# Strassen's block products for the FFN up product of the last eight token tiles, with the converted weights kept in DRAM

## The chip, the core and the metric

The kernel runs on one core of a Trainium2 chip. The metric is the device time of one execution in microseconds (us). Four engines compute: TensorE (PE in the profile: matrix products, 128 x 128 weights against up to 512 columns, results in eight PSUM banks), VectorE (DVE), ScalarE (ACT) and GpSimd (POOL). All DMAs are issued from SyncE's queue (SP). Each engine works through its own instructions in the order in which they stand and waits at semaphores for the others.

## The reference

Attention with capped scores for 48 heads, then one FFN over 1792 tokens (14 tiles of 128), with a residual:

```python
scores = cap * np.tanh(scale * np.matmul(q, k.transpose(0, 1, 3, 2)) / cap)
attn = np.exp(scores - np.max(scores, axis=-1, keepdims=True))
attn = attn / (np.sum(attn, axis=-1, keepdims=True) + 1e-09)
x = np.matmul(attn, v)                     # (4, 12, 448, 64), all fp32
x = x.transpose(0, 2, 1, 3).reshape(4, 448, 768)
xn = (x - mean) / np.sqrt(var + 1e-06) * g_ln
out = x + np.maximum(xn @ w_ch1, 0.0) @ w_ch2   # 768 -> 3072 -> 768
```

q, k and v are fp32; the two weights are float64 and come as pairs of 32-bit words.

## The kernel before

**Products in two halves.** The FFN products need fp32 accuracy from a faster fp32r product, so each operand is split into a high part h and a rest l, and each product is three matmuls: h with h, l with h, h with l (L818 to L820 for the up product, L843 to L845 for the down product).

**Tiles and groups.** The hidden layer is worked through in 24 chunks of 128 (`fc`), the 768 input columns in 6 chunks (`CC`). The 14 token tiles are in four groups: A0 and A1 (3 tiles, 384 columns each), C0 and C1 (4 tiles, 512 columns each). `up` makes one chunk of the hidden layer for one group (18 matmuls), takes it out of PSUM with a ReLU on ACT (L823) and makes its rest on DVE (L825). `down` multiplies 2 or 4 such chunks with the second weight into a bank of 128 x 384, and DVE adds the bank to the tokens (L847).

**Weights.** Every chunk of either weight is one DMA of 768 KB (L764); ACT or POOL scale it (L769, L770), POOL and DVE put the words together (L773, L776, L778), ACT and DVE make h and l (L372, L379). This is done twice for each of the 48 chunks: `ffn(0, ...)` runs over the 24 chunks for A0 and, from chunk 8 on, also A1, while the attention of the later heads is still going on; `ffn(1, ...)` runs over them again for C0 and C1, and for A1 in the first 8.

**Norm.** `norm` makes, for one group, the statistics (L705, L707), the inverse root (L717 to L719), the normed tokens xn (L726), their transposes on PE (L734), and the h and l parts (L739, L743).

**What sets the order.** Every operation is recorded with an engine, a cost, a due time and the buffers that it needs. `Order.emit` goes through time with the given costs and lets each engine take the earliest due operation that is ready and whose buffers are free. So each engine's order is fixed when the kernel is built. Buffers of a kind are slots: a PSUM `bank` has 8, and a tag limits how many of them one use may hold.

## Time and profile before

| | |
|---|---|
| runs shown | 923.58 us median of 3: 920.82, 923.58, 1266.4 |
| profiled execution, first to last instruction | 920.0 us; its own device time is not listed, the shortest run is 0.8 us above this span, the median 3.6 us |
| busy | PE 902.9 us (98%), DVE 608.0 (66%), ACT 388.5 (42%), POOL 131.3 (14%) |
| DMA | 109.59 MB, mean 119 GB/s, 37.9% of 16 engines |
| granted TensorE clock | 0.999 |

A share of busy time is an average. The rows by stretch show which engine has no time left in which part, and the waits which engine another one stands still for. Busy PE time is a union of overlapping matmuls, so what one matmul costs in a row of them is read from the count in a stretch, not from its own duration.

### The profile page before, as it was taken

What the parts mean: (1) busy time and instruction counts of PE and PEld (TensorE: products, weight loads), DVE (VectorE), ACT (ScalarE), POOL (GpSimd) and SP (SyncE); (2) the same over time, 40 slices, a digit from 0 to 9 for tenths busy, and PEclk for the clock granted to TensorE, in tenths of its full rate; (3) what the DMA queues carried; (4) which work ended last, traced back from release to release, by engine and by line L of the source; (5) the groups of instructions that cost most, each with busy time, mean ns of one, the idle gap of its engine ahead of it and who ended that gap; (6) DMA issues with size and microseconds to landing.
All of it is one profiled execution on the core that took longest, in us unless ns stands there. A gap on an engine that the chain in (4) does not pass through costs nothing.

```text
span 920.0 us, 12465 instructions
## 1 busy us (share of the span) xinstructions
PE 902.9 (98%) x4886; PEld 746.8 (81%) x4886; DVE 608.0 (66%) x926; ACT 388.5 (42%) x553; POOL 131.3 (14%) x162
## 2 busy tenths in 40 slices
PE   8899999999999999999999999999999999999997
PEld 5337674877787777879989898989889899899896
DVE  2998788987775848569989373736473573663622
ACT  7865777765555574732442212111330430330400
POOL 2434111211110101011211010100020110110100
PEclk9999999999999999999999999999999999999999
DMA  9781655475434343236333130302241241240212
GB/s 230 217 238 50 188 166 153 122 229 137 151 116 158 107 130 117 92 104 260 117 107 110 54 112 28 110 30 82 78 144 63 71 170 35 97 144 35 70 61 80
DMA packets 34260, 109.59 MB, mean 119 GB/s; under 512 B 5008, under 2 KB 17808, under 8 KB 34192
## 3 DMA queue, kind: packets, MB, share of 16 engines
q1 hardware_dynamic: 34192, 108.71, 37.9%
q8 instruction: 40, 0.66, 0.3%
q14 instruction: 28, 0.23, 0.1%
HBM read 100.04 MB, written 8.65 MB: 118 GB/s over the span
## 4 chain that ended last, share of the span: by engine, by line
PE 90%; DVE 5%; ACT 2%; DMA 1%; issue 1%; POOL 1%; DVEq 0%; ACTq 0%
PE bank L818 13%; PE bank L843 13%; PE bank L845 12%; PE bank L819 12%; PE bank L844 12%; PE bank L820 12%; PE bank L575 5%; PE bank L424 5%; DMA raw<-in_w_dram 1%; PE bank L734 1%; PE bank L591 1%; ACT e L609 1%; DVE l L379 1%; PE bank L546 1%; PE bank L506 1%
## 5 line engine op out<-in xcount | busy, mean ns | idle before, releaser
L843 PE MATMUL bank<-h,hh 128*128 128x384 f32 x672 | 225.7, 336 | 0.2 <-DVE r L535 0.2
L845 PE MATMUL bank<-h,hl 128*128 128x384 f32 x672 | 224.6, 334 | 0.0
L844 PE MATMUL bank<-l,hh 128*128 128x384 f32 x672 | 224.5, 334 | 0.0
L847 DVE TENSOR_TENSOR x<-bank,x 128x384 f32<-128x384 f32 x272 | 146.5, 551 | 100.2 <-PE bank L845 99.5
L773 POOL TENSOR_SCALAR raw<-raw 128x768 f32<-128x768 f32 x96 | 104.3, 1087 | 622.3 <-ACT c L769 621.9
L372 ACT ACTIVATE h<-c 128x768 fp32r<-128x768 f32 x88 | 73.8, 843 | 186.6 <-PE bank L845 99.6
L843 PEld LDWEIGHTS bank<-h,hh 128*128 128x128 f32 x672 | 126.1, 188 | 6.8 <-issue 2.7
L844 PEld LDWEIGHTS bank<-l,hh 128*128 128x128 f32 x672 | 126.1, 188 | 0.2
L845 PEld LDWEIGHTS bank<-h,hl 128*128 128x128 f32 x672 | 126.1, 188 | 0.0
L823 ACT ACTIVATE hh<-bank 128x384 fp32r<-128x384 f32 (+1 forms) x96 | 52.2, 543 | 174.8 <-PE bank L820 174.7
L776 DVE SCALAR_TENSOR_TENSOR raw<-raw 128x768 int32<-128x768 int32 x96 | 92.6, 965 | 38.2 <-POOL raw L773 37.9
L769 ACT ACTIVATE c<-raw 128x768 f32<-128x768 f32 x88 | 79.8, 908 | 87.5 <-DMA raw<-in_w_dram 44.6
L818 PE MATMUL bank<-hC,h 128*128 128x512 f32 x288 | 113.9, 396 | 0.0
L825 DVE SCALAR_TENSOR_TENSOR hl<-bank,hh 128x384 fp32r<-128x384 f32 (+1 forms) x96 | 59.4, 619 | 82.3 <-ACT hh L823 82.1
L820 PE MATMUL bank<-hC,l 128*128 128x512 f32 x288 | 113.8, 395 | 0.0
L819 PE MATMUL bank<-lC,h 128*128 128x512 f32 x288 | 113.7, 395 | 0.0
L379 DVE TENSOR_TENSOR l<-c,h 128x768 fp32r<-128x768 f32 x96 | 94.0, 981 | 28.6 <-ACT h L372 26.9
L778 DVE SCALAR_TENSOR_TENSOR c<-c,raw 128x768 int32<-128x768 int32 x96 | 102.2, 1064 | 2.3
L818 PE MATMUL bank<-hA,h 128*128 128x384 f32 x288 | 100.6, 349 | 0.2 <-ACT e L609 0.2
L819 PE MATMUL bank<-lA,h 128*128 128x384 f32 x288 | 97.5, 339 | 0.0
L820 PE MATMUL bank<-hA,l 128*128 128x384 f32 x288 | 97.4, 338 | 0.0
L609 ACT ACTIVATE e<-bank,sc 128x448 f32<-128x448 f32 x144 | 81.1, 647 | 25.9 <-PE bank L575 25.9
(76 smaller groups left out, 914.0 us busy)
## 6 DMA issues: line engine op xcount, KB each, us to landing
raw<-in_w_dram SPq DMA_DIRECT2D x96, 768.0 KB, 4.5
d<-in_kq_dram SPq DMA_DIRECT2D x48, 224.0 KB, 6.2
v<-in_v_dram SPq DMA_DIRECT2D x24, 227.5 KB, 5.5
out_dram<-x SPq DMA_DIRECT2D x28, 192.0 KB, 1.9
v<-in_v_dram SPq DMA_DIRECT2D x24, 195.0 KB, 5.4
x<-xd SPq DMA_DIRECT2D x8, 384.0 KB, 7.8
xd<-a SPq DMA_DIRECT2D x21, 128.0 KB, 3.4
xd<-a SPq DMA_DIRECT2D x6, 64.0 KB, 2.0
```

What stands on the lines that cost most here:

```text
L379: self.eng(e).tensor_tensor(out=out, in0=in_, in1=high.bitcast(F32), op=ALU.subtract)
L609: add({"A": ACTP(S) + 93}, lambda e: nc.scalar.activation(tiles[p].ap[:, k, j] if p < 2 else er.ap[:, k], z.ap[:, :S], AF.Tanh, scale=self ...
L773: add(on("sg", G=POOL1(DM), V=VEC1(DM)), lambda e: nc.gpsimd.tensor_scalar(f(hi()), f(hi()), 0.0, 1.0, op0=ALU.mult, op1=ALU.mult) if e == ...
L776: add({"V": VEC2(DM)}, lambda e: nc.vector.scalar_tensor_tensor(hi(), lo(), 29, hi(), op0=ALU.logical_shift_right, op1=ALU.bitwise_or), wr ...
L778: add({"V": VEC2(DM)}, lambda e: nc.vector.scalar_tensor_tensor(c.ap, c.ap, 3, hi(), op0=ALU.logical_shift_left, op1=ALU.bitwise_or), read ...
L818: nc.tensor.matmul(ps.ap[:, :n], lhsT=w1h.ap[:, wc], rhs=xh.ap[:, c], start=(c == 0), stop=False)
L819: nc.tensor.matmul(ps.ap[:, :n], lhsT=w1h.ap[:, wc], rhs=xl.ap[:, c], start=False, stop=False)
L820: nc.tensor.matmul(ps.ap[:, :n], lhsT=w1l.ap[:, wc], rhs=xh.ap[:, c], start=False, stop=(c == CC - 1))
L843: nc.tensor.matmul(o, lhsT=h[0].ap[:, mc], rhs=w[0].ap[:, hc], start=(f == 0), stop=False)
L844: nc.tensor.matmul(o, lhsT=h[0].ap[:, mc], rhs=w[1].ap[:, hc], start=False, stop=False)
L845: nc.tensor.matmul(o, lhsT=h[1].ap[:, mc], rhs=w[0].ap[:, hc], start=False, stop=(f == last))
L847: add({"V": VEC2(HALF)}, lambda e, t=t, ps=ps, hc=hc: nc.vector.tensor_tensor(out=self.x(t)[:, hc], in0=ps.ap[:, :HALF], in1=self.x(t)[:, ...
```

## The change

The groups C0 and C1 get their up product as a 2 x 2 block product: two hidden chunks by two halves of the 768 inputs by two token groups. Strassen's form in Winograd's variant makes it from 7 block products of 9 matmuls (`stage`, 12 times) where the plain form has 8. The seven token operands (named 11, 21, 22, 1, 2, 3, 4, tiles `X1` to `X7` in that order) are made once in `blocks`; the seven weight operands are made in each stage from fp32 weights. Partial results are taken aside by ACT (`aside`, L1054) and added on DVE (`plus`, L1059). Each stage is followed by its own down product over 2 chunks instead of 4.

Each weight chunk is converted once. Its fp32 form is written to DRAM (`keep`, L839) and read back (`fetch`, L844) where it is needed again: for the first 8 chunks of A1, which get a phase of their own between the two others, and for the 12 stages. C's tokens are normed in place and read from DRAM a second time for the residual. The statistics of the tokens that go to DRAM are taken piece by piece in `finish` (L584) before they are stored. The pools are laid out anew, so the order comes out differently in the attention part too.

```diff
--- before.py
+++ after.py
 HALF = DM // 2
 NA = 6
 GROUPS = dict(A0=(0, 3), A1=(3, 3), C0=(6, 4), C1=(10, 4))
-FBS = [2, 4]
-HBS = [4, 8]
-W2S = [3, 4]
+FB = 2
+HB = 4
 WRAP = 8
+SLOTS = 8
+KH = CC // 2
+NE = KH * 128
+TOK = 512
 VEC1 = lambda n: 60 + 0.75 * n
...
-    w1=20000, w2=3000, evac=2000, cstep=15600, cnorm=10000, load=20000, zpad=3000, rush=30000, ahead=20000,
+    w1=20000, w2=3000, evac=2000, bstep=6300, cstep=31200, cnorm=10000, load=20000, zpad=3000, rush=30000, ahead=20000,
+    again=12000, down=16000, chunk=8000, blocks=4000,
...
+                add({"V": 330}, lambda e, dst=dst, tl=tl, p=p: nc.vector.bn_stats(
+                    self.stats.ap[p, tl % SLOTS, h0 // GROUP], dst()), reads=writes,
+                    writes=[(self.stats, tl % SLOTS, h0 // GROUP, p.start)], due=due)
...
+        self.keep((w, fc), lambda: f(c.ap), [c], due)
+        self.tail = op
         return h, l
-    def ffn(self, gi, hp, t0, step):
-
-        fc0 = 0
-        while fc0 < FC:
-            early = fc0 < WRAP
-            keys = (["A0"] if early else ["A0", "A1"]) if gi == 0 else (["C0", "C1", "A1"] if early else ["C0", "C1"])
-            n = FBS[0] if early else FBS[gi]
-            end = {"A0": FC, "A1": WRAP if gi else FC * (WRAP == 0), "C0": FC, "C1": FC}
-            due2 = t0 + (fc0 + 0.5 * n) * step
+    def again(self, w, fc, due, tag="cq"):
+
+        nc, add = self.nc, self.add
+        c = self.buf("wp", tag, [128, DM], F32)
+        op = self.fetch((w, fc), lambda: c.ap, [c], due, [self.gate, *self.rear])
+        self.fetched.append(op)
+        h, l = self.pair(w, fc)
+        self.split(h, l, c, due)
+        return h, l
+
+    def keep(self, key, ap, reads, due):
+        to = self.kept[key]
+        self.add({"S": 550}, lambda e: self.nc.sync.dma_start(out=to.bitcast(F32), in_=ap().bitcast(F32)),
+                 reads=reads, writes=[("kept", *key)], due=due, dma=128 * to.shape[1] * 4)
+
+    def fetch(self, key, ap, writes, due, after, allocs=()):
+        of = self.kept[key]
+        return self.add({"S": 550}, lambda e: self.nc.sync.dma_start(out=ap(), in_=of),
+                        reads=[("kept", *key)], writes=writes, due=due - PLAN["again"], dma=128 * of.shape[1] * 4,
+                        after=after, allocs=allocs)
+
+    def split(self, h, l, src, due, cols=None, key=None, n=DM):
+
+        key = src if key is None else key
+        at = lambda: src.ap if cols is None else src.ap[:, cols]
+        self.add({"A": ACTS(n)}, lambda e: self.round(e, h.ap, at().bitcast(F32)), reads=[key], writes=[h.key], due=due)
+        return self.add({"V": VEC2(n)}, lambda e: self.rest(e, l.ap, at().bitcast(F32), h.ap), reads=[key, h.key], writes=[l.key], due=due)
+
...
+    def blocks(self, due):
...
+        T = {n: buf(p, f"X{n}", [128, 2, KH, TOK], F32R, 1)
+             for p, ns in (("xo1", "1234"), ("xo2", "567")) for n in ns}
+        self.T = T = dict(zip(("11", "21", "22", "1", "2", "3", "4"), T.values()))
+        begin = due
...
+            b11, b12, b22, t3, b21 = (buf("y", "y", [128, TOK], F32) for _ in range(5))
+            first = [turned(b11, 0, 0, (b12, b22, t3))]
+            keep("11", b11)
+            turned(b12, 0, 1, after=first)
+            turned(b22, 1, 1, after=first)
+            keep("22", b22)
+            less(t3, b22, b12)
+            keep("3", t3)
+            less(b12, b12, b11)
+            keep("1", b12)
+            less(b22, b22, b12)
+            keep("2", b22)
+            turned(b21, 1, 0, after=first)
+            keep("21", b21)
+            less(b21, b21, b22)
+            keep("4", b21)
+
+    def stage(self, q, due, done):
+        nc, add, buf = self.nc, self.add, self.buf
+        A, T = ALU.add, ALU.subtract
+        wdue = due - PLAN["w1"]
+        blk = [buf("wp", "blk", [128, DM], F32) for _ in range(2)]
+        sums = [buf("wp", "sum", [128, 2, NE], F32) for _ in range(2)]
+        for i in range(2):
+            self.fetch((0, 2 * q + i), lambda i=i: blk[i].ap, [blk[i]], wdue, self.rear, blk + sums)
+        half = lambda i, j: lambda: blk[i].ap[:, j * NE:j * NE + NE]
+        S = [Part(sums[i // 2], i % 2) for i in range(4)]
+        look = lambda p: lambda: p.ap
+        def mix(out, a, ka, b, kb, op):
+            add({"V": VEC2(NE)}, lambda e: nc.vector.tensor_tensor(out=out.ap, in0=a(), in1=b(), op=op),
+                reads=[ka, kb], writes=[out.key], due=wdue)
+        mix(S[0], half(1, 0), blk[1], half(1, 1), blk[1], A)
+        mix(S[1], look(S[0]), S[0].key, half(0, 0), blk[0], T)
+        mix(S[2], half(0, 0), blk[0], half(1, 0), blk[1], T)
+        mix(S[3], half(0, 1), blk[0], look(S[1]), S[1].key, T)
+        def operand(src, key, cols=None):
+            o = buf("wp", "opd", [128, 2, NE], F32R)
+            h, l = Part(o, 0), Part(o, 1)
+            self.split(h, l, src, wdue, cols=cols, key=key, n=NE)
+            return h, l
+        first, second = slice(0, NE), slice(NE, 2 * NE)
+        W = {}
+        W[1] = operand(blk[0], blk[0], first)
+        W[5] = operand(S[0], S[0].key)
+        W[6] = operand(S[1], S[1].key)
+        W[2] = operand(blk[0], blk[0], second)
+        W[7] = operand(S[2], S[2].key)
+        W[4] = operand(blk[1], blk[1], second)
+        W[3] = operand(S[3], S[3].key)
+        X = {1: "11", 2: "21", 3: "22", 4: "4", 5: "1", 6: "2", 7: "3"}
+        def product(n, ps, start):
+            wh, wl = W[n]
+            x = self.T[X[n]]
+            def mm(e):
+                for c in range(KH):
+                    wc = slice(c * 128, c * 128 + 128)
+                    o = dict(stop=False, skip_group_check=not start)
+                    nc.tensor.matmul(ps.ap, lhsT=wh.ap[:, wc], rhs=x.ap[:, 0, c], start=start and c == 0, **o)
+                    nc.tensor.matmul(ps.ap, lhsT=wh.ap[:, wc], rhs=x.ap[:, 1, c], start=False, **o)
+                    o["stop"] = c == KH - 1
+                    nc.tensor.matmul(ps.ap, lhsT=wl.ap[:, wc], rhs=x.ap[:, 0, c], start=False, **o)
+            add({"T": 9 * MM(TOK)}, mm, reads=[wh.key, wl.key] + [(x, i, c) for i in range(2) for c in range(KH)],
+                writes=[ps], due=due)
+        def aside(ps):
+            y = buf("y", "y", [128, TOK], F32)
+            add({"A": ACTP(TOK)}, lambda e: nc.scalar.activation(y.ap, ps.ap, AF.Copy), reads=[ps], writes=[y],
+                due=due - PLAN["evac"])
+            return y
+        def plus(y, ps):
+            add({"V": VEC2(TOK)}, lambda e: nc.vector.tensor_tensor(out=y.ap, in0=ps.ap, in1=y.ap, op=ALU.add),
+                reads=[ps], writes=[y], due=due - PLAN["evac"])
+        def hidden(src):
+            hh, hl = (buf("hc", "hh", [128, TOK], F32R, 6), buf("hc", "hl", [128, TOK], F32R, 6))
+            self.bend(src, hh, hl, TOK, due - PLAN["evac"])
+            return hh, hl
+        bank = lambda: buf("ps", "u", [128, 512], F32)
+        pa, pb, pc = bank(), bank(), bank()
+        product(1, pa, True)
+        u1 = aside(pa)
+        product(5, pc, True)
+        product(6, pa, False)
+        u2 = aside(pa)
+        product(2, pb, True)
+        plus(u1, pb)
+        h11 = hidden(u1)
+        product(7, pa, False)
+        u3 = aside(pa)
+        plus(u3, pc)
+        h22 = hidden(u3)
+        product(4, pa, False)
+        h21 = hidden(pa)
+        product(3, pc, False)
+        plus(u2, pc)
+        h12 = hidden(u2)
+        ws = [self.again(1, 2 * q + i, due, "cw") for i in range(2)]
+        for tl in range(NA, NT) if not q else ():
+            self.load_x(tl, due, self.fetched[-2:])
+        self.down("C0", [h11, h21], ws, due + PLAN["down"], done)
+        self.down("C1", [h12, h22], ws, due + PLAN["down"], done)
...
         def swap1(e):
             self.close("xna", "att")
-            for n in ("xnc", "xtC", "xC"):
+            for n in ("xC", "y", "xo1"):
                 self.open(n, side="right")
+            self.grow("wp", "c", 2, None)
+
+        def swap2(e):
+            self.close("raw", "xA0", "xtA0")
+            for n in ("xo2", "wc"):
+                self.open(n, side="right")
+            self.grow("wp", "c", 2, "wc")
+
+        def swap3(e):
+            self.close("ha", "xA1", "xtA1")
+            for n in ("hc", "wd"):
+                self.open(n)
+            self.grow("wp", "q", 5, "wd")
         self.gate = self.add({"P": 0}, swap1, after=self.uses("xna", "att"), due=0)
-        for k in range(2):
-            self.norm(f"C{k}", "xtC", "xnc", AEND - PLAN["cnorm"])
-        self.ffn(0, "ha", A0, ASTEP)
-
-        def swap2(e):
-            self.close("ha", "w2a", "xA0", "xtA0")
-            for n in ("hc", "w2c"):
-                self.open(n)
-
-        self.gate2 = self.add({"P": 0}, swap2, after=self.uses("ha", "w2a", "xA0", "xtA0"), due=0)
-        self.ffn(1, "hc", AEND, PLAN["cstep"])
+        self.ffn(range(0, FC, FB), self.weight, lambda fc: ["A0"] + ["A1"] * (fc >= WRAP), lambda fc: A0 + fc * ASTEP, "ha")
+        self.gate2 = self.add({"P": 0}, swap2, after=self.uses("xA0", "xtA0", "raw") + [self.gate], due=0)
+        self.ffn(range(0, WRAP, FB), self.again, lambda fc: ["A1"], lambda fc: AEND + fc * BSTEP, "ha")
+        self.rear = self.fetched[-2:]
+        self.gate3 = self.add({"P": 0}, swap3, after=self.uses("ha", "xA1", "xtA1") + [self.gate2], due=0)
+        self.blocks(AEND + PLAN["blocks"])
+        self.last(BEND, PLAN["cstep"])
+        for o in self.order.ops:
+            for b in o.bufs:
+                g = {"xC": self.gate, "y": self.gate, "xo1": self.gate, "xo2": self.gate2, "hc": self.gate3}.get(b.pool)
+                if g is not None and g not in o.after:
+                    o.after.add(g)
+                    g.outs.append(o)
+                    o.left += 1
         self.planned = self.order.emit(self.realize)
-        self.close("ps", "w2c", "hc", "xC", "xtC", "xnc", "xA1", "xtA1", "xd", "small")
+        self.close("ps", "wd", "hc", "wc", "xo2", "xo1", "y", "xC", "xd", "small")
 @with_exitstack
```

Three places of the orders follow. First PE at the norm of A1, where the last transposes of the second batch of heads are followed by a down product and then by the transposes of xn. Before:

```order
L845 MATMUL bank_205<-h_415,hl_859 128x384
L575 MATMUL bank_215<-d_74 128x448
L575 MATMUL bank_224<-d_74 128x448
L575 MATMUL bank_204<-d_74 128x448
L575 MATMUL bank_230<-d_74 128x448
L818 MATMUL bank_216<-hA_620,h_67 128x384
...
L734 MATMUL bank_229<-ident,xn_596 128x128
```

The same place in the change (L910 to L912 are the down product, L762 the transposes):

```order
L912 MATMUL bank_265<-w_69,hl_910 128x384
L762 MATMUL bank_281<-ident,xn_675 128x128
...
L762 MATMUL bank_266<-ident,xn_675 128x128
...
L762 MATMUL bank_274<-ident,xn_675 128x128
...
L762 MATMUL bank_253<-ident,xn_675 128x128
...
L762 MATMUL bank_275<-ident,xn_675 128x128
...
L762 MATMUL bank_254<-ident,xn_675 128x128
```

Four score products and twelve matmuls of an up product stood between the down product and the first transposes; now nothing stands there, and four of the six banks of transposes are banks of that down product.

DVE at the same place of the change, from the first product with 1/sum (L580) to the evictions of that down product (L915):

```order
L580 TENSOR_TENSOR a_1365<-bank_265,r_519 128x256
...
L815 SCALAR_TENSOR_TENSOR raw_261<-raw_261 128x768
L733 TENSOR_SCALAR mv_1374<-mv_1374 128x3
L471 TENSOR_TENSOR d_317<-e_255 128x896
L817 SCALAR_TENSOR_TENSOR c_63<-c_63,raw_261 128x768
...
L754 TENSOR_SCALAR xn_680<-x_433,mv_1374 128x768
L403 TENSOR_TENSOR q_66<-c_63,q_65 128x768
L915 TENSOR_TENSOR x_418<-bank_274,x_418 128x384
L915 TENSOR_TENSOR x_418<-bank_253,x_418 128x384
L915 TENSOR_TENSOR x_418<-bank_275,x_418 128x384
L915 TENSOR_TENSOR x_418<-bank_254,x_418 128x384
```

And before:

```order
L556 TENSOR_TENSOR a_1312<-bank_205,r_475 128x256
...
L847 TENSOR_TENSOR x_368<-bank_215,x_368 128x384
...
L447 TENSOR_TENSOR d_266<-e_206 128x896
...
L847 TENSOR_TENSOR x_368<-bank_204,x_368 128x384
...
L847 TENSOR_TENSOR x_368<-bank_216,x_368 128x384
...
L847 TENSOR_TENSOR x_368<-bank_229,x_368 128x384
L726 TENSOR_SCALAR xn_596<-x_386,mv_1324 128x768
```

Four evictions stood ahead of xn; now two weight conversions stand there, and the evictions follow xn.

PE in a stage of the change that stands for the later ones, the first of nine matmuls of each block product (X tile 4, 5, 2, 6, 1, 7, 3; the one with X1 belongs to the next stage):

```order
L1044 MATMUL bank_274<-X_3780,q_4429 128x512
...
L1044 MATMUL bank_265<-X_3799,q_66 128x512
...
L1044 MATMUL bank_266<-X_3771,q_4342 128x512
...
L1044 MATMUL bank_265<-X_3765,q_4415 128x512
...
L1044 MATMUL bank_281<-X_3738,q_4399 128x512
...
L1044 MATMUL bank_265<-X_3823,q_67 128x512
...
L1044 MATMUL bank_274<-X_3759,q_65 128x512
```

Between two products that go on in one bank there is one other product each time, where before an up product of C ran its 18 matmuls in one go. The 96 matmuls of the stage's down product follow.

## Rows read from the trace of the kernel before

**Rows 1.** The page: span, and busy time, share and instructions of each engine.

```profile
span 920.0 us, 12465 instructions
PE 902.9 (98%) x4886; PEld 746.8 (81%) x4886; DVE 608.0 (66%) x926; ACT 388.5 (42%) x553; POOL 131.3 (14%) x162
```

**Rows 2.** Windows: stretch, busy us (count) by engine, granted clock, DMA share, GB/s.

```profile
core 0: us, PE busy (x) PEld busy (x) DVE busy (x) ACT busy (x) POOL busy (x), PEclk, DMA share, GB/s
0.00:60.00 60.00, 54.28 (x300) 25.21 (x302) 42.17 (x66) 43.26 (x61) 21.75 (x40) 1.00 0.86 229
60.00:120.00 60.00, 57.34 (x314) 39.27 (x313) 49.39 (x81) 41.64 (x62) 14.91 (x17) 1.00 0.50 144
120.00:420.00 300.00, 297.95 (x1717) 229.07 (x1716) 223.42 (x335) 179.54 (x262) 43.58 (x54) 1.00 0.45 135
420.00:460.00 40.00, 40.00 (x240) 39.96 (x239) 39.67 (x90) 13.20 (x20) 8.27 (x7) 1.00 0.54 197
500.00:900.00 400.00, 400.00 (x2034) 363.64 (x2033) 213.32 (x301) 93.94 (x128) 37.41 (x39) 1.00 0.24 82
```

**Rows 3.** Windows of a stretch of down product alone, and of C's up product alone.

```profile
680.00:700.00 20.00, 20.00 (x117) 20.00 (x116) 12.54 (x18) 2.88 (x4) 1.76 (x2) 1.00 0.46 156
720.00:740.00 20.00, 20.00 (x87) 16.07 (x86) 13.64 (x16) 10.28 (x14) 3.00 (x3) 1.00 0.39 127
```

**Rows 4.** Groups by form: names, shapes, count | busy us, mean ns | idle before, releaser.

```profile
L818 PE MATMUL bank<-hC,h 128*128 128x512 f32 x288 | 113.9, 396 | 0.0
...
L847 DVE TENSOR_TENSOR x<-bank,x 128x384 f32<-128x384 f32 x272 | 146.5, 551 | 100.2 <-PE bank L845 99.5
...
L778 DVE SCALAR_TENSOR_TENSOR c<-c,raw 128x768 int32<-128x768 int32 x96 | 102.2, 1064 | 2.3
...
L379 DVE TENSOR_TENSOR l<-c,h 128x768 fp32r<-128x768 f32 x96 | 94.0, 981 | 28.6 <-ACT h L372 26.9 <-POOL h L376 1.4
...
L825 DVE SCALAR_TENSOR_TENSOR hl<-bank,hh 128x512 fp32r<-128x512 f32 x48 | 33.0, 687 | 50.9 <-ACT hh L823 50.9
...
L823 ACT ACTIVATE hh<-bank 128x512 fp32r<-128x512 f32 x48 | 28.6, 596 | 122.5 <-PE bank L820 122.5
```

**Rows 5.** Timeline of PE at A1's norm: start us, us, line, tiles, count.

```profile
161.28 0.44 PE L843 MATMUL bank<-h,hh 128*128 128x384 f32 x1 [0.18 <-DVE r L535]
...
167.75 1.77 PE L575 MATMUL bank<-d 64*128 64x448 f32 x8
...
171.68 1.47 PE L734 MATMUL bank<-ident,xn 128*128 128x128 f32 x12
```

**Rows 6.** Timeline of DVE at the same place, and two busy runs of equal instructions later.

```profile
161.00 0.23 DVE L535 TENSOR_SCALAR r<-bank,eps 128x16 f32<-128x16 f32 x1
...
161.62 1.22 DVE L556 TENSOR_TENSOR x<-bank,r 64x256 f32<-64x256 f32 x3
...
169.50 2.07 DVE L726 TENSOR_SCALAR xn<-x,mv 128x768 f32<-128x768 f32 x3
...
449.31 1.00 DVE L847 TENSOR_TENSOR x<-bank,x 128x384 f32<-128x384 f32 x2
...
458.23 4.04 DVE L743 SCALAR_TENSOR_TENSOR lC<-bank,gt,hC 128x512 fp32r<-128x512 f32 x6
```

**Rows 7.** DMA issues: size of each, median us from issue to landing.

```profile
raw<-in_w_dram SPq DMA_DIRECT2D x96, 768.0 KB, 4.5
...
xd<-a SPq DMA_DIRECT2D x21, 128.0 KB, 3.4
```

**Rows 8.** Timelines of the end: last eviction on DVE, last stores on SP's queue.

```profile
913.32 0.56 DVE L847 TENSOR_TENSOR x<-bank,x 128x384 f32<-128x384 f32 x1 [1.52 <-PE bank L845]
...
907.66 6.58 SPq L852 DMA_DIRECT2D out_dram<-x  x5
```

More of the change, by code (lines that the diff above doesn't have):

```diff
@@ L94, in __init__, with ap @@
         self.users, self.ap, self.last, self.share, self.since = 0, None, 0.0, None, 0.0
+class Part:
+    def __init__(self, buf, *at):
+        self.buf, self.at = buf, at
+        self.key = (buf, *at) if at else buf
+    @property
+    def ap(self):
+        ap = self.buf.ap
+        for n, a in enumerate(self.at):
+            ap = ap[:, a]
+        return ap
 class Op:
-    __slots__ = ("engine", "cost", "fn", "due", "bufs", "left", "outs", "ready", "end", "dma", "seq", "wait")
+    __slots__ = ("engine", "cost", "fn", "due", "bufs", "left", "outs", "ready", "end", "dma", "seq", "wait", "after")
 class Order:
@@ L124, in add @@
         deps.discard(op)
-        op.left, op.outs, op.ready, op.end, op.wait = len(deps), [], 0.0, None, None
+        op.left, op.outs, op.ready, op.end, op.wait, op.after = len(deps), [], 0.0, None, None, deps
         for d in deps:
@@ L138, in emit @@
         ready = {e: [] for e in free}
-        slots = {(0, *k): list(range(n)) for k, n in self.places.items()}
+        slots = self.slots = {(0, *k): list(range(n)) for k, n in self.places.items()}
         slots.update({(1, *k): list(range(n)) for k, n in self.limits.items()})
@@ L722, in norm @@
         add({"V": 700}, rstd, writes=[mv], due=due)
+        return mv
+    def norm(self, key, xtp, xnp, due):
+        nc, add, buf = self.nc, self.add, self.buf
+        t0, nt = GROUPS[key]
+        tiles = range(t0, t0 + nt)
+        n = len(tiles) * 128
+        xh = buf(xtp, f"h{key}", [128, CC, n], F32R, 1)
+        xl = buf(xtp, f"l{key}", [128, CC, n], F32R, 1)
+        self.xT[key] = xh, xl
+        xns = []
+        mv = self.statistics(key, due)
         for m, tl in enumerate(tiles):
-            xn = buf(xnp, "xn", [128, DM], F32, 4 if late else 3)
+            xn = buf(xnp, "xn", [128, DM], F32, 3)
             xns.append(xn)
@@ L727, in norm @@
                 xn.ap, self.x(tl), mv.ap[:, m, 0:1], mv.ap[:, m, 2:3], op0=ALU.subtract, op1=ALU.mult),
-                reads=[self.xkey(tl), mv], writes=[xn], due=due, after=hold)
+                reads=[self.xkey(tl), mv], writes=[xn], due=due)
         for c in range(CC):
@@ new lines, in ffn @@
+    def ffn(self, fcs, weight, keys, due, hp):
+        for fc0 in fcs:
+            ws, hs = [], {}
+            ks = keys(fc0)
+            for f in range(FB):
+                t = due(fc0 + 0.5 * f)
+                ws.append([weight(w, fc0 + f, t - PLAN[f"w{w + 1}"]) for w in range(2)])
+                for key in ks:
+                    hs[key, f] = self.up(key, ws[f][0], hp, t)
+            for key in ks:
+                last = WRAP if key == "A1" else FC
+                self.down(key, [hs[key, f] for f in range(FB)], [w[1] for w in ws], due(fc0 + 0.5 * FB), fc0 + FB == last)
@@ L845, in mm @@
                         nc.tensor.matmul(o, lhsT=h[1].ap[:, mc], rhs=w[0].ap[:, hc], start=False, stop=(f == last))
-                    add({"T": 3 * MM(HALF)}, mm, reads=[x for g in (*hs, *ws) for x in g], writes=[ps], due=due, after=hold)
+                    add({"T": 3 * MM(HALF)}, mm, reads=[*(x for g in hs for x in g), *(x.key for g in ws for x in g)],
+                        writes=[ps], due=due)
                 add({"V": VEC2(HALF)}, lambda e, t=t, ps=ps, hc=hc: nc.vector.tensor_tensor(
@@ new lines, in load_x, with last @@
+    def load_x(self, tl, due, hold):
+        self.add({"S": 550}, lambda e: self.nc.sync.dma_start(out=self.x(tl), in_=self.xd[tl]),
+                 reads=[("xd", tl, c) for c in self.xd_parts(tl)], writes=[self.xkey(tl)], due=due, dma=128 * DM * 4, after=hold)
+    def last(self, t0, step):
+        for q in range(FC // 2):
+            self.stage(q, t0 + q * step, q == FC // 2 - 1)
+    def stage(self, q, due, done):
+        nc, add, buf = self.nc, self.add, self.buf
+        A, T = ALU.add, ALU.subtract
[33 more added lines that the diff above has]
+            def mm(e):
+                for c in range(KH):
+                    wc = slice(c * 128, c * 128 + 128)
[5 more added lines that the diff above has]
+            add({"T": 9 * MM(TOK)}, mm, reads=[wh.key, wl.key] + [(x, i, c) for i in range(2) for c in range(KH)],
+                writes=[ps], due=due)
+        def aside(ps):
[9 more added lines that the diff above has]
+            self.bend(src, hh, hl, TOK, due - PLAN["evac"])
+            return hh, hl
+        bank = lambda: buf("ps", "u", [128, 512], F32)
[22 more added lines that the diff above has]
+        self.down("C1", [h12, h22], ws, due + PLAN["down"], done)
@@ L895, in run @@
         self.xd = {tl: self.pools["xd"].tile([128, DM], F32, name=f"xd{tl}") for tl in range(NA, NT)}
[L896 removed]
+        self.kept, self.fetched, self.rear = {}, [], []
+        for fc in range(FC):
+            for w in range(2):
+                self.kept[w, fc] = self.pools["xd"].tile([128, DM], F32, name=f"kept{w}{fc}")
+        for n in ("xtA1", "xA1", "ha", "xtA0", "xA0", "raw"):
             self.open(n)
```

147 lines of the change are left out of this document (87 added, 60 removed).

## The prediction, made before the changed kernel ran

> **What bounds the kernel now.** I read the page first, for the engine that is never free: PE is busy 902.9 of 920.0 us, DVE 608.0 [rows 1]. A mean hides the stretches, so the windows come next [rows 2]. In them the reader is to see two kernels in one. Up to 120 us PE stands still for 5.7 and 2.7 us, DMA is at a share of 0.86 in the first 60 us, and attention sets the pace. From 120 us PE is busy 297.95 of 300 us, then 40.00 of 40 and 400.00 of 400: from there to the tail the time is the number of matmuls times the price of one. DVE is also full from 420 to 460 us (39.67 of 40) and PE does not stand still there: a full DVE costs nothing as long as nothing on PE is close behind it. The granted clock is 1.00, 2.4 GHz, in every one of these stretches.
>
> The price of a matmul is not its own duration, since matmuls overlap. A stretch of down product holds 117 of 384 columns in 20 us, so 0.171 us each; a stretch of C's up product 87 of 512 columns, so 0.230 us each [rows 3], while the group by form says 396 ns [rows 4].
>
> **What the change takes away.** C's up product has 6 input chunks x 3 matmuls x 2 groups x 24 hidden chunks = 864 matmuls of 512 columns, 288 on each of three lines [rows 4]. The change has 7 products x 9 x 12 stages = 756. 108 fewer x 0.230 = **24.8 us less** on an engine that has no free time there. All other PE work keeps its count: 2016 down matmuls, 864 of A's up product, 84 transposes.
>
> The Trainium skill (TensorE: Matmul & The Clock Gate, Back-to-back issue gap) gives about 131 ns as the sustained spacing of weight load and matmul at 512 columns. By it the 108 would be worth an estimated 14.1 us and not 24.8; the stretch with 87 in 20 us does not agree with it, so the row is taken.
>
> The second conversion of 48 weight chunks goes too: on DVE two operations each (at 0.88 us in a queue), about 84 us, on POOL 48 operations, and 48 loads of 768 KB. In the C part DVE and POOL bounded nothing (213.32 and 37.41 of 400 us [rows 2]), so this gives no time; it pays for what comes in.
>
> **What it adds to a stage, and why I count that at nothing.** Neighbours in DVE's queue overlap by 0.1 us: two evictions take 1.00 us [rows 6] and not twice 0.551 [rows 4]. Without that discount a stage costs DVE 16 evictions x 0.551, 4 rests of the hidden layer and 3 additions x 0.687 [rows 4], 7 rests and 4 mixes of 384 columns x 0.551 (nearest row: the eviction, equal width), and 2 rests x 0.981: 8.8 + 4.8 + 6.1 + 2.0 = 21.7 us. PE needs 63 x 0.230 + 96 x 0.171 = 30.9 us. ACT has 7 copies x about 0.5 us, 7 x 0.596 [rows 4] and 2 x 0.9: 9.5 us. PE still bounds the stage. Within it, a product that goes on in a bank waits for ACT's copy of that bank (0.6 us), and one other product of 9 x 0.230 = 2.07 us lies between, as the order shows; the last product waits for copy and addition, 1.3 us, behind two products. If DVE or ACT come over 1.4 us late, this cover is gone (a rival below). Four reads of 384 KB for 31 us are 50 GB/s, against the 82 GB/s that this part moved before.
>
> **A1's norm: a wait that comes in.** Here the order makes me add time. Before, DVE needs from L535 at 161.00 to the end of the third xn at 171.57, 10.6 us [rows 6], and PE fills nearly the same time, from 161.28 to the first transposes at 171.68, with 36 down matmuls, four score products at 167.75 (1.7 us) and 12 matmuls of an up product (2.1 us) [rows 5]. In the change PE has the 36 down matmuls alone and is through at 167.7. DVE's chain swaps four evictions (4 x 0.45) for two conversions (2 x 0.88) and one more statistic (0.33): 10.9 us, the last xn at 171.9, the first, 1.3 us earlier, at 170.6. Then a second thing: four of the six transposes' banks still hold the down product, and its evictions stand behind xn and a rest: 171.9 + 0.9 + 4 x 0.45 = 174.6 for the fourth. The last three transposes end at about 175.0. Of the 7.3 us from 167.7, the transposes themselves fill 18 x 0.12 = 2.2 (12 take 1.47 [rows 5]). So PE stands still 5.1 us, and the next score products wait for one more eviction and the first rest of the new operands, some 0.9 us: **+6 us** (3 if DVE comes to L535 a few us sooner, 7 if the banks cost more).
>
> **The phase between.** A1's 8 chunks on their own and the making of the seven token operands now meet. From the first transposes to the first block product PE has 108 up and 108 down matmuls x 0.171 and 48 transposes x 0.12: 42.7 us. DVE's order has, from the first X rest to the last rest of A1, 33 operations of 512 columns from SBUF, 9 of 768, 12 evictions and 6 rests of 384. The 512s have no row: between 0.45 for 384 and 0.88 for 768, below 4.04 / 6 = 0.67 from PSUM [rows 6], I take 0.6: 19.8 + 7.9 + 18 x 0.45 = 35.8 us. DVE is 84% full and PE just behind it with small covers. From 420 to 460 us a fuller DVE cost nothing [rows 2]; here the first block products need the last of 21 rests. I take **+2 us** (0 to 6).
>
> **DRAM copies in the attention part.** 48 writes of 384 KB (18.9 MB) join the queue. SP's order puts each behind the load whose buffer comes free at the same DVE operation, so the queue waits there anyway and loses one issue. Six writes fall into the first 60 us: 2.4 MB at 229 / 0.86 = 266 GB/s are 8.9 us of DMA time, and 0.14 x 60 = 8.4 us are free [rows 2]: just full. From 60 us half the DMA time is free. A write's landing time (3.4 us for 128 KB [rows 7]) is hidden, as the buffer has two slots and a weight comes every 7.5 us. The attention part's order changes as well; PE has 8.4 us of idle time to win there at most [rows 2]. I take **0** (-4 to +5). The 27 pieces of statistics come to 0.33 us each on DVE and replace 24 between 420 and 460 us: 0.
>
> **The tail.** PE's last product, one eviction (913.32 + 0.56) and the last store to 920.0 [rows 8] stay. The 16 stores come every 1.03 us and not 2.06, which is 190 GB/s, below 266: 0 (0 to +1).
>
> **Sum:** 920.0 - 24.8 + 6 + 2 = 903.2 us of span. The runs shown lie 0.8 to 3.6 us above the span of 920.0; with 2.2 that is **905.4 us**, 2.0% below the median of 923.58. Faster by over 2% begins below 905.1, slower above 942.1; 2% is about what a measurement of this kernel can tell from no change.
>
> **Rivals.**
> - **Every new wait is hidden.** DVE reaches L535 early enough, since it has fewer evictions ahead, and operands come in time. Against it: the cover at A1's norm is gone from the order. 920.0 - 24.8 + 2.2 = 897 us. Chance 0.12.
> - **The joins eat the gain.** DMA is full for the first 60 us and DVE for the phase between; each of the bounds at its upper end gives +7 +6 +5 +1 and so 914 + 2 = 916 us (909 to 925). For it: the share of 0.86 [rows 2]. Against: from 60 us there is room. Chance 0.22.
> - **Slower: the product chain waits on ACT and DVE.** A stage has three copies aside that the next product in the bank needs, and an eviction run on DVE can hold the additions up. With no cover at all a stage would pay 3 x 0.6 for copies, 0.69 for the addition ahead of the last product and 0.6 + 0.69 for the last hidden chunk ahead of the down product: 3.8 us x 12 = 45 us, so 950 us. It decides from 3.3 us a stage (905 + 12 x 3.1 = 942). For it: an up product of C before had no such wait. Against: the covers of 2.07 us, and DVE 70% full. Chance 0.07.
>
> **How the numbers follow.** The forecast, 899 to 909, has 0.59, the rivals 0.12, 0.22 and 0.07. The range of 896 to 920 holds the forecast, nearly all of the first rival and two thirds of the second. Faster: the first rival and about half of the forecast, 0.42. Slower: 0.07. Within 2%: 0.51. The forecast lies on the bound, which is why no side has most of it.
>
> **What would show it.** Matmuls of 512 columns: 756 where there were 864, at 0.23 us. PE idle for 5 to 6 us at A1's second set of transposes, put down to DVE. From 500 us PE full, apart from 1 to 3 us at the first block product. Conversions on DVE halved, its share in C between 60 and 70%. DMA: 19 MB written more in the attention part. I am wrong if PE waits at regular intervals in the stages (slower rival), if the idle time lies before 120 us (DMA), or if the spacing of the block products is not 0.23 us.

## The result, and the profile after

The changed kernel takes 905.31 us (median of 4 runs, 903.13 to 906.28). The kernel before beside it took 919.99, 920.82 and 923.58 us, and 1266.4 in one disturbed run that is left out. The ratio is 0.982 [0.980, 0.984]: faster by 1.8%, clear of the noise and inside the 2% that the prediction counts as no change. The forecast was 905.4. Its profiled execution took 905.73 us, with a span of 903.9: 16.1 us less than [rows 1].

The page, span and engines, and two of its groups with their counts:

```profile
span 903.9 us, 12581 instructions
...
PE 883.8 (98%) x4778; PEld 730.7 (81%) x4778; DVE 641.1 (71%) x1078; ACT 411.0 (45%) x638; POOL 80.5 (9%) x114
...
HBM read 90.60 MB, written 27.53 MB: 131 GB/s over the span
...
L915 DVE TENSOR_TENSOR x<-bank,x 128x384 f32<-128x384 f32 x336 | 182.5, 553 | 80.0 <-PE bank L912 79.5
...
L1044 PE MATMUL bank<-X,q 128*128 128x512 f32 x252 | 99.7, 396 | 1.4 <-ACT y L1054 1.4
```

252 matmuls on each of three lines are the 756 of the forecast, and 64 more evictions (336 for 272) come from down products over 2 chunks and not 4. Of the 27.53 MB written 18.7 are the copies (8.85 are left in thin_keeping below). DVE has more to do and is still not the bound. The windows that answer to [rows 2]:

```profile
core 0: us, PE busy (x) PEld busy (x) DVE busy (x) ACT busy (x) POOL busy (x), PEclk, DMA share, GB/s
0.00:60.00 60.00, 54.83 (x300) 24.82 (x302) 41.14 (x65) 45.08 (x65) 20.34 (x38) 1.00 0.92 240
60.00:120.00 60.00, 57.09 (x317) 40.71 (x318) 48.70 (x81) 37.79 (x56) 14.76 (x18) 0.97 0.60 177
120.00:420.00 300.00, 295.02 (x1668) 224.33 (x1668) 228.48 (x356) 179.25 (x260) 42.45 (x56) 0.99 0.63 184
420.00:460.00 40.00, 40.00 (x232) 40.00 (x230) 29.90 (x61) 9.39 (x14) 2.97 (x3) 1.00 0.55 185
...
500.00:900.00 400.00, 396.89 (x2025) 361.07 (x2023) 259.43 (x463) 114.13 (x203) 0.00 (x0) 1.00 0.20 64
```

Two things are to be seen. Up to 420 us PE stands still for 5.17 + 2.91 + 4.98 = 13.06 us, where [rows 2] gives 5.72 + 2.66 + 2.05 = 10.43. And the granted clock, 1.00 in all of [rows 2], is now 0.97 and 0.99 in two stretches. The last transposes of the attention part show how much both cost together. Their row in the trace of before:

```profile
412.36 1.04 PE L546 MATMUL bank<-ident,b 128*128 128x128 f32 x8
```

and after the change:

```profile
419.85 1.04 PE L570 MATMUL bank<-ident,b 128*128 128x128 f32 x8
```

Up to these transposes PE has made the same matmuls in both kernels, line by line. So the attention part lost 7.5 us, and from there to the end the change won 507.6 - 484.1 = 23.6 us (rounded). The sum is the 16.1 of the span.

**Where the 7.5 us went.** PE's waits (engine, line, for whom: us in all, times, longest), the five longest:

```profile
PE bank L912 <- DVE hl L894: 2.3, 2, 1.9
PE bank L448 <- ACT e L640: 2.1, 4, 0.8
PE bank L762 <- DVE xn L754: 2.1, 3, 1.6
PE bank L570 <- issue: 1.6, 1, 1.6
PE bank L1044 <- ACT y L1054: 1.4, 2, 0.7
```

L762 is the transposes of the norm, here A1's. PE's timeline there (start us, us, line, tiles, count, the wait ahead of it), from the end of the 36 down matmuls:

```profile
169.10 0.34 PE L912 MATMUL bank<-w,hl 128*128 128x384 f32 x1
171.07 0.30 PE L762 MATMUL bank<-ident,xn 128*128 128x128 f32 x1 [1.64 <-DVE xn L754]
171.57 0.33 PE L762 MATMUL bank<-ident,xn 128*128 128x128 f32 x1 [0.20 <-DVE xn L754]
172.16 0.65 PE L762 MATMUL bank<-ident,xn 128*128 128x128 f32 x4 [0.26 <-DVE xn L754]
173.50 2.65 PE L762 MATMUL bank<-ident,xn 128*128 128x128 f32 x12 [0.68 <-DVE x L915]
176.07 2.30 PE L602 MATMUL bank<-d 64*128 64x448 f32 x8
178.31 0.45 PE L881 MATMUL bank<-hA,q 128*128 128x384 f32 x1
```

The wait for xn and then for the evictions x is the one forecast, place and releasers included. From 169.4 to 176.15 are 6.7 us for 2.2 us of work, so 4.5 lost. But the clock fell as well, three times in this execution, each time after PE had stood still. Windows of 2 us at the first of them and at the norm:

```profile
104.00:106.00 2.00, 1.11 (x5) 1.12 (x6) 2.00 (x6) 1.93 (x4) 0.00 (x0) 0.88 0.66 65
106.00:108.00 2.00, 2.00 (x8) 2.00 (x7) 2.00 (x4) 2.00 (x3) 0.00 (x0) 0.50 0.68 246
...
172.00:174.00 2.00, 1.16 (x8) 0.77 (x8) 2.00 (x5) 1.05 (x2) 0.00 (x0) 0.94 0.66 267
174.00:176.00 2.00, 2.00 (x10) 1.74 (x9) 2.00 (x5) 1.78 (x4) 0.31 (x1) 0.50 0.00 0
```

A clock of 0.50 is 1.2 GHz. The third place is 160 to 163 us, behind the 1.6 us of L570. In all three places PE is "busy" for longer than its work needs. At 103 us it is 1.6 us (the last section has the rows). At 158 us it is 1.5: from the first L570 to the last down matmul are 9.77 us, and 8.32 in thin_keeping below, where the clock stayed up there. At the norm it is 2.2: 6.1 us of busy time from 171.07 to 178.31 for some 3.9 us of work. With 13.06 - 10.43 = 2.6 us more standing still this makes 7.9, about the 7.5. How much of the 2.2 is the clock is asked by hold_clock below.

The wait at 158 us itself is not new. Before the change PE stood still there as well, and the granted clock stayed at 1.00:

```profile
158.79 0.63 PE L532 MATMUL bank<-ident,b 128*128 128x128 f32 x4 [1.28 <-ACT b L479]
...
160.66 0.44 PE L546 MATMUL bank<-ident,b 128*128 128x128 f32 x2 [0.59 <-ACT e L609]
```

After the change, ACT's rows and then PE's:

```profile
157.96 0.84 ACT L396 ACTIVATE w<-c 128x768 fp32r<-128x768 f32 x1 [3.66 <-DVE c L817]
158.71 1.39 ACT L503 ACTIVATE b<-bank 128x448 f32<-128x448 f32 x3
...
159.33 0.30 PE L570 MATMUL bank<-ident,b 128*128 128x128 f32 x1 [1.55 <-issue]
```

The transposes turn b, which ACT copies out of PSUM (L503) only after a conversion (L396) that waits 3.66 us for DVE. What is new at this place is the fall of the clock behind the wait.

### The profile page after: what moved, and what is told of

Its sections match the earlier page's. It is cut to its first block, busy times and chain, and to the rows that moved or that the text cites. A ratio compares the mean times of both kernels' runs of the same rounds, so it can differ in the third digit from the quotient of the medians.

```text
span 903.9 us, 12581 instructions
## 1 busy us (share of the span) xinstructions
PE 883.8 (98%) x4778; PEld 730.7 (81%) x4778; DVE 641.1 (71%) x1078; ACT 411.0 (45%) x638; POOL 80.5 (9%) x114
## 3 DMA queue, kind: packets, MB, share of 16 engines
HBM read 90.60 MB, written 27.53 MB: 131 GB/s over the span
## 4 chain that ended last, share of the span: by engine, by line
PE 82%; DVE 11%; issue 2%; DMA 2%; POOL 1%; ACT 1%; SPq 0%; DVEq 0%; POOLq 0%; ACTq 0%
PE bank L912 12%; PE bank L910 12%; PE bank L911 12%; PE bank L1044 7%; PE bank L1047 7%; PE bank L1045 7%; PE bank L881 5%; PE bank L448 5%; PE bank L883 4%; PE bank L882 4%; PE bank L602 4%; DVE x L915 1%; DVE X L403 1%; DVE c L817 1%; PE bank L570 1%
## 5 line engine op out<-in xcount | busy, mean ns | idle before, releaser
L915 DVE TENSOR_TENSOR x<-bank,x 128x384 f32<-128x384 f32 x336 | 182.5, 553 | 80.0 <-PE bank L912 79.5
L912 PE MATMUL bank<-w,hl 128*128 128x384 f32 x672 | 227.6, 339 | 2.3 <-DVE hl L894 2.3
L910 PE MATMUL bank<-w,hh 128*128 128x384 f32 x672 | 228.4, 340 | 0.0
L911 PE MATMUL bank<-w,hh 128*128 128x384 f32 x672 | 227.1, 338 | 0.0
L910 PEld LDWEIGHTS bank<-w,hh 128*128 128x128 f32 x672 | 127.2, 189 | 5.2 <-ACT e L636 2.0
L912 PEld LDWEIGHTS bank<-w,hl 128*128 128x128 f32 x672 | 126.9, 189 | 3.3 <-DVE hl L894 3.3
L911 PEld LDWEIGHTS bank<-w,hh 128*128 128x128 f32 x672 | 127.1, 189 | 0.6
L1044 PE MATMUL bank<-X,q 128*128 128x512 f32 x252 | 99.7, 396 | 1.4 <-ACT y L1054 1.4
L881 PE MATMUL bank<-hA,q 128*128 128x384 f32 x288 | 100.8, 350 | 0.0
L1045 PE MATMUL bank<-X,q 128*128 128x512 f32 x252 | 99.6, 395 | 0.0
L1047 PE MATMUL bank<-X,q 128*128 128x512 f32 x252 | 99.5, 395 | 0.0
L883 PE MATMUL bank<-hA,q 128*128 128x384 f32 x288 | 97.6, 339 | 0.3 <-DVE q L403 0.3
L882 PE MATMUL bank<-lA,q 128*128 128x384 f32 x288 | 97.5, 338 | 0.0
L396 ACT ACTIVATE w<-d 128x768 fp32r<-128x768 f32 x13 | 11.0, 847 | 160.7 <-issue 133.4
L403 DVE TENSOR_TENSOR q<-c,q 128x384 fp32r<-128x384 f32 (+1 forms) x86 | 61.1, 710 | 24.5 <-ACT q L396 24.0
L894 DVE SCALAR_TENSOR_TENSOR hl<-bank,hh 128x384 fp32r<-128x384 f32 (+1 forms) x60 | 34.5, 578 | 48.1 <-ACT hh L892 48.1
L640 ACT ACTIVATE e<-e,capt 128x1344 f32<-128x1344 f32 x48 | 66.3, 1431 | 0.0
L602 PE MATMUL bank<-d 64*128 64x448 f32 x288 | 65.7, 569 | 0.5 <-DVE x L580 0.4
L881 PEld LDWEIGHTS bank<-hA,q 128*128 128x128 f32 x288 | 54.0, 188 | 14.9 <-issue 8.0
L396 ACT ACTIVATE q<-c 128x384 fp32r<-128x384 f32 (+1 forms) x82 | 50.2, 613 | 33.7 <-PE bank L1045 12.6
```

Source lines behind the costliest of these rows:

```text
L602: self.nc.tensor.matmul(z[k].ap[:, :S], lhsT=kqs[p].ap[rows[k], l, 128 * j:128 * j + 128], rhs=kqs[p].ap[rows[k], r], start=True, stop=True)
L881: nc.tensor.matmul(ps.ap[:, :n], lhsT=w1h.ap[:, wc], rhs=xh.ap[:, c], start=(c == 0), stop=False)
L882: nc.tensor.matmul(ps.ap[:, :n], lhsT=w1h.ap[:, wc], rhs=xl.ap[:, c], start=False, stop=False)
L883: nc.tensor.matmul(ps.ap[:, :n], lhsT=w1l.ap[:, wc], rhs=xh.ap[:, c], start=False, stop=(c == CC - 1))
L910: nc.tensor.matmul(o, lhsT=h[0].ap[:, mc], rhs=w[0].ap[:, hc], start=(f == 0), stop=False)
L911: nc.tensor.matmul(o, lhsT=h[0].ap[:, mc], rhs=w[1].ap[:, hc], start=False, stop=False)
```

## The experiments

Each is an edit of the changed kernel, except where said. Times of before beside them: 921.1 us for the first four, 920.7 for the others.

**eight_products: the plain form in the same frame.** Is the gain the count, or the conversions that are no longer made twice?

```diff
-        product(1, pa, True)
-        u1 = aside(pa)
...
-        plus(u2, pc)
-        h12 = hidden(u2)
+        h = {}
+        for n in range(2):
+            for i in range(2):
+                ps = bank()
+                for j in range(2):
+                    product(i, j, n, ps, j == 0)
+                h[i, n] = hidden(ps)
```

> Everything of the change stays (weights converted once, kept in DRAM, A1's own phase), but each stage makes its hidden layer from the plain 2 x 2 block product: 8 block products of 9 matmuls, no mixes of weights, no copies aside, no additions; four token operands and not seven. Theory (the gain is the count): 108 matmuls of 512 columns come back, +24.8 us at 0.230, less 1 to 3 us for the waits at the first block products that go: 926 to 930 us, so slower than the kernel before by 0.4 to 0.9%. Rival (the gain is in the conversions and loads that are no longer made twice, and block products are worth little): 905 to 912 us. In the trace the theory wants 864 matmuls of 512 columns, the wait at A1's norm unchanged, and PE with no idle time from 510 us to the tail.

Measured: 927.0 us, 1.006 [1.004, 1.009] of before. The theory holds. A stage's length is read from ACT: the first copy or ReLU of one stage to that of the next. After the change:

```profile
747.41 0.60 ACT L1054 ACTIVATE y<-bank 128x512 f32<-128x512 f32 x1 [1.75 <-PE bank L1047]
...
778.75 0.60 ACT L1054 ACTIVATE y<-bank 128x512 f32<-128x512 f32 x1 [1.75 <-PE bank L1047]
```

and with eight products:

```profile
722.83 0.60 ACT L892 ACTIVATE hh<-bank 128x512 fp32r<-128x512 f32 x1 [2.61 <-PE bank L1014]
...
756.28 0.60 ACT L892 ACTIVATE hh<-bank 128x512 fp32r<-128x512 f32 x1 [2.62 <-PE bank L1014]
```

31.34 and 33.45 us: 9 matmuls are worth 2.10 us, 0.233 each, and twelve stages 25.2. In the whole time 21.7 of this is seen (927.0 - 905.3). The profiled executions also differ ahead of the stages: with eight products the clock fell once in the attention part and not three times, and the last transposes stand 2.1 us earlier (417.71). From the first block product to the last matmul, where that plays no part, the difference is 407.3 - 384.1 = 23.3 us; stage_alone below tells where the other 1.9 go.

**norm_ahead: the wait at A1's norm.**

```diff
-        add({"G": 800}, lambda e: nc.gpsimd.tensor_tensor(
+        add({"G": 5000}, lambda e: nc.gpsimd.tensor_tensor(
...
-        mv = self.statistics(key, due)
+        mv = self.statistics(key, due - 40000)
...
-                reads=[self.xkey(tl), mv], writes=[xn], due=due)
+                reads=[self.xkey(tl), mv], writes=[xn], due=due - 40000)
```

> Only the order: A1's statistics and normed tokens get an earlier due time and the inverse root a larger planned cost, so that the order puts a score product and the 18 matmuls of an up product between the 36 down matmuls and A1's transposes, and the evictions between the steps of the norm. Theory (the 6 us of the norm are a wait without cover, and the low clock behind it comes from that wait): PE's idle time from 165 to 180 us falls from about 4 us to 2 to 3, the granted clock stays at 1.00 there (1.6 us), and the time is 900 to 903 us. Rival (the wait only moves: DVE's work in front of the transposes is the bound and PE waits as long elsewhere): 904 to 907 us, with as much PE idle time between 160 and 200 us as before the edit.

Measured: 898.98 us (898.12 to 901.05), 0.976 [0.974, 0.978] of before: 6.3 us less than the changed kernel, more than the theory gave. Its timeline of PE, with the first row at 103 us, the second at 158 us and the others at the norm:

```profile
103.88 0.44 PE L912 MATMUL bank<-w,hl 128*128 128x384 f32 x1 [0.18 <-DVE hl L894]
...
155.51 0.47 PE L570 MATMUL bank<-ident,b 128*128 128x128 f32 x2
...
166.05 1.02 PE L602 MATMUL bank<-d 64*128 64x448 f32 x2 [0.58 <-DVE x L915]
167.47 0.42 PE L881 MATMUL bank<-hA,q 128*128 128x384 f32 x1 [0.41 <-DVE mv L728]
...
168.25 0.52 PE L882 MATMUL bank<-lA,q 128*128 128x384 f32 x1
168.57 0.53 PE L883 MATMUL bank<-hA,q 128*128 128x384 f32 x1
...
172.25 2.13 PE L762 MATMUL bank<-ident,xn 128*128 128x128 f32 x18
```

All 18 transposes run without a wait behind an up product. The same edit also moved work at the two other places: of the wait of 1.9 us at 103 us 0.18 are left, and that of 1.6 us at 158 us is gone. The last transposes of the attention part stand here:

```profile
412.49 1.04 PE L570 MATMUL bank<-ident,b 128*128 128x128 f32 x8
```

So another order gives back the 7.4 us (419.85 - 412.49), all of them: they were the price of the order, with the falls of the clock behind its waits. The run moves all three places at once and does not price them one by one. The expectation of a steady clock at the norm failed: PE waits twice ahead of L881, and from 168.3 to 171.5 us its matmuls start 0.32 us apart (168.25 and 168.57 in the rows) and not 0.17.

**thin_keeping: the copies to DRAM.**

```diff
-    ... dma_start(out=to.bitcast(F32), in_=ap().bitcast(F32)),
+    ... dma_start(out=to.bitcast(F32)[:, :8], in_=ap().bitcast(F32)[:, :8]),
...
-        of = self.kept[key]
+        of = self.kq[2 * key[1] + key[0]][:, :DM]
```

> The order stays as it is. Each of the 48 writes of converted weights to DRAM moves 8 columns of 768 (the rest isn't written), and the reads fetch 384 KB of the input kq in place of the kept weights; so 18.7 MB of writes fall away and every wait stays. Theory (the writes cost nothing beside the rest): 904 to 906 us. Rival (DMA is full in the first 60 us and the writes hold k, q, v and weights back): PE idle in the first 60 us falls from 5 to 3 us, landing times of kq and v go back to about 6.2 and 5.5 us, and the waits at 103 and 158 us get shorter: 898 to 902 us.

This kernel leaves 18.7 MB of the copies unwritten and later reads input in their place. Measured: 905.76 us (905.0 to 906.27), the same as the changed kernel. The transfers did become faster; its rows, size and median us to landing, and its first window:

```profile
d<-in_kq_dram SPq DMA_DIRECT2D x48, 224.0 KB, 5.6
...
v<-in_v_dram SPq DMA_DIRECT2D x24, 227.5 KB, 5.0
```

```profile
0.00:60.00 60.00, 54.69 (x300) 24.46 (x302) 41.64 (x65) 45.26 (x65) 20.95 (x38) 1.00 0.84 220
```

In the changed kernel these landed after 7.3 and 6.3 us, and DMA's share was 0.92. PE stands still just as long (5.31 and 5.17 us). The term of 0 was right, and the rival's first half too: transfers do get slower, but no time is lost by it.

**stage_alone: the covers in a stage.**

```diff
-        product(1, pa, True)
+        product(1, pa, True, [self.third] if q else ())
...
-        product(3, pc, False)
+        self.third = product(3, pc, False)
```

(`product` hands the list on as the `after` of its operation and returns the operation.)

> One added condition: a stage's first block product is made after the last block product of the stage before it, so it no longer lies between the two products that go on in one bank (7 and 4 in the order of the code). That takes one cover of 2.07 us away per stage, nothing else. Theory (this cover hides the copy that ACT takes aside): PE waits 0.6 to 0.9 us for ACT in each stage, 12 x 0.75 = 9 us, so 912 to 917 us, and the wait is put down to y of the copy. Rival (covers don't decide, since PE is behind anyway or the copy is early enough): under 1.5 us in all, 904 to 907 us.

Measured: 916.09 us (915.49 to 917.42), 10.8 more than the changed kernel: the theory. Its waits for the copies:

```profile
PE bank L1044 <- ACT y L1054: 9.0, 13, 0.7
```

13 waits of 0.69 where there were 2. A stage is 32.28 us long (783.44 - 751.16 between its copies) and not 31.34, so a wait of 0.69 us costs 0.95: the wait also ends the overlap with the matmul ahead, and the second matmul behind it starts after 0.34 us and not 0.23 (760.20 and 760.54). Eleven stages at 0.95 are 10.5 of the 10.8 us. The changed kernel pays this price twice (529.84 and 877.67 us, in the first and the last stage, which have no neighbour to borrow from): 1.9 us, the difference between the 25.2 and the 23.3 above.

**hold_clock: is it the clock that makes the work behind the norm slow?**

```diff
             def turn(e, c=c, ps=ps):
+                fill = self.xT["A0"][0].ap
+                for _ in range({0: 10, 1: 4}.get(c, 0) if key == "A1" else 0):
+                    nc.tensor.matmul(ps.ap[:, :n], lhsT=fill[:, 0, :128], rhs=fill[:, 0], start=True, stop=True)
```

> The order and every wait of the changed kernel stay. Into the idle time at A1's norm come 14 matmuls of 384 columns whose results are written over by the transposes: 10 ahead of the first bank's transposes, 4 ahead of the second's (2.4 us of PE work in a stretch where PE stood still for 3 us). Theory (the slow transposes and score products behind the norm are slow because the clock fell while PE stood still): the granted clock is 1.00 from 170 to 180 us, the last 12 transposes take 1.5 to 1.7 us where they took 2.65, and the first score products behind them 1.77 where they took 2.30; the time is up to 1.6 us shorter, 903 to 906 us. Rival (they are slow for their own reasons, such as banks in use by DVE): 2.6 and 2.3 us as before, and 905 to 908 us with the added work.

Measured: 905.14 us (903.74 to 906.26), no change, and in the range of either theory; the rows decide. The clock did stay up in the profiled execution, and the work stayed slow (line numbers from L762 on are 3 higher here):

```profile
172.00:174.00 2.00, 1.89 (x12) 1.50 (x13) 2.00 (x5) 1.07 (x2) 0.00 (x0) 1.00 0.61 246
174.00:176.00 2.00, 2.00 (x12) 1.31 (x13) 2.00 (x5) 2.00 (x5) 0.51 (x1) 1.00 0.00 0
```

```profile
172.98 2.40 PE L765 MATMUL bank<-ident,xn 128*128 128x128 f32 x15
175.31 2.58 PE L602 MATMUL bank<-d 64*128 64x448 f32 x8
177.82 0.45 PE L884 MATMUL bank<-hA,q 128*128 128x384 f32 x1
```

From the first transpose to the first up product are 6.89 us and not 7.24. My theory falls for this place: of the 2.2 us the low clock costs 0.3 to 0.4. What is left for the rest is the pace at which DVE, busy 2.00 of 2.00 us in these windows, frees the banks; in norm_ahead, where the evictions of the down product stand ahead, the 18 transposes take 2.13 us. No run shows this pace by itself. stage_alone, whose clock happened not to fall at the norm, needs 6.80 us without any filling; so this run does not show either that filling is what holds the clock.

**eight_norm_ahead: the plain form with the mended order.** The edits of eight_products and norm_ahead together.

> The plain block product (8 of 9 matmuls a stage) together with the order that mended A1's norm. It has the weights converted once and kept in DRAM, and A1's own phase, but not Strassen's form and not the norm's wait. Theory (the fewer conversions and loads are worth no time, and the 5.9 us by which the plain block product was slower than the kernel before were the norm's wait and the clock behind it): 919 to 923 us, the same as the kernel before within 0.3%; and 21 to 25 us more than the same order with seven products (899.0). Rival (keeping weights in DRAM and A1's own phase cost time of their own): 924 to 927 us. Second rival (the fewer conversions do bring time once the norm is out of the way): under 917 us.

Measured: 921.9 us (920.89 to 922.4), 1.001 [1.000, 1.002] of before, and 22.9 us more than with seven products. Weights converted once and a phase of its own for A1 are worth no time and cost none in the whole. The last transposes stand at 412.30 us, as before the change.

**norm_and_w2: what is left of the phase between.** norm_ahead, with one number more:

```diff
-    w1=20000, w2=3000, evac=2000,
+    w1=20000, w2=5000, evac=2000,
```

> The order that mended A1's norm, and one more number of the plan: the second weight's due time 5 us ahead of its use where it was 3. It is to take the waits for rests out of the phase between A0's and C's products (0.4 us at the last down product of A1, and the time that PE loses at the first block products). Theory (what is left of the term for the phase between is 1 to 2 us, DVE being just late there): 896.5 to 898.5 us. Rival (those waits were covered): 898 to 900 us, the same as without it.

Measured: 898.22 us (897.89 to 899.02), 0.976 [0.974, 0.977] of before. Against 898.98 the time alone can't tell it from norm_ahead. The trace can: from the last transposes of the attention part (412.01) to the first block product (505.88) it needs 93.87 us, as eight_norm_ahead does (412.30 to 506.17), where norm_ahead needs 94.55 (412.49 to 507.04) and the changed kernel 94.52 (419.85 to 514.37). The phase between had cost 0.65 us, less than the 1 to 2 of the theory. Of the kernels measured this is the fastest, though not proven faster than norm_ahead.

## Why the prediction was right, and where it was not

- **The count, -24.8:** right, and as a price per matmul: 25.2 measured in the stages. The estimate of 14.1 us, which came from the Trainium skill (TensorE: Matmul & The Clock Gate, Back-to-back issue gap), is out: 2.10 us per block product of 9 leaves no room for 0.131 us a matmul.
- **A1's norm, +6:** mechanism, place and releasers as forecast: xn 10.7 us after L559 (10.9 forecast), then four evictions. At the norm itself 4.5 us show, and 1.0 more was hidden since the down matmuls ahead ran partly at 1.2 GHz; thin_keeping, where they did not, waits 2.61 us for xn and not 1.64. Of the 5.1 us of idle time forecast 2.8 came as idle time (1.64 + 0.20 + 0.26 + 0.68), and 1.7 as transposes that take longer than the 0.12 us each that I gave them.
- **The attention part, 0:** right for DMA (thin_keeping), wrong for the order. The step that took the changed order there at 0 looked at idle time to win before 120 us and not at waits to come: at 103 us a down product waits 1.9 us for a rest (L894) that DVE makes behind two steps of a weight conversion (L815, L817) and two statistics; in norm_ahead it stands ahead of the second step. At 158 us the wait was there before the change too, and only the lower clock behind it is new. The clock was taken to stay at 1.00, as in all of [rows 2]; that was the other failed step. Norm and attention together lost 7.5 us against the 6 forecast.
- **The phase between, +2:** 0.65.
- **The stages, 0:** nearly. Ten of twelve have full cover, the first and the last pay 0.95 each, 1.9 in all. That 31.34 us is more than the 30.9 forecast is no wait: the counts in [rows 3] put a matmul 1.4% too low, in both forms.
- **The tail, 0:** 1.6 us shorter. From the end of the last matmul to the end of the span are 5.1 us in the profiled execution, and 6.7 in that of before; in the runs above 5.4 to 6.1. No run asks why.
- **The sum:** -25.2 + 1.9 + 0.65 + 7.5 - 1.6 = -16.8 against -16.1 measured. The missing 0.6 is no matter of the seven products: from the last transposes to the last matmul eight_norm_ahead, too, takes 0.6 us longer than the kernel before (501.2 and 500.6). Its cause is open.

That the time came within 0.1 us of the forecast is luck. The count, the tail and the phase between came out 0.4, 1.6 and 1.35 us better than their terms, the attention part with the norm 1.5 worse, the stages 1.9 worse, and 0.6 is open. These errors leave 0.7 us (a span of 903.9 for 903.2), and the step from span to time, 1.8 for 2.2, takes more than half of that away; the median lies another 0.4 below the profiled execution.

The rivals: **every new wait hidden** (897) is what norm_and_w2 comes to, 898.2; it was the order that missed it. **The joins eat the gain** put its losses, beside the norm, into full DMA, which costs nothing (thin_keeping), and into a full DVE in the phase between, which costs 0.65; the loss of 7.5 us came from the order of the attention part. **The slower rival** has a price of the right kind (stage_alone: 0.95 us a stage for one cover gone, where the rival took 0.6 a copy), but its condition isn't met, since the order puts the next stage's first product between the two that share a bank.

## What to carry to other kernels

Where an engine has no free time, as PE here, a change is worth its count times the spacing in a dense stretch; the conversions and transfers that it saved on other engines were worth nothing. Then look at what the new order does to the stretches that the change did not mean to touch: here two waits and the lower clock in three places ate 7.5 of 25 us, and two due times and one planned cost gave them back. Ask of every wait what was queued ahead of the late operation on the engine that is waited for.
